# Sliding-window attention and a two-layer MLP on one core: an earlier cast of V, one pair's casts on another engine, masks as factors, and one pair moved by a slot

## Chip, cores, metric

One core of a Trainium2 chip (runs e1 to e9 on one chip, e10 to e13 on another). The metric is the device time of one execution in microseconds (us), measured some 2 us longer than the span of the trace of the same execution. The engines are TensorE (PE in the profile, PEld its weight loads), VectorE (DVE), ScalarE (ACT), GpSimd (POOL) and SyncE (SP, which here only issues DMAs).

## The reference

Eight batches of eight heads, sequence 576, head size 64. Each query sees the 64 latest keys. The attention's output, as 4608 tokens by 512, goes through two matrices with `h - tanh(h)` between.

```python
rel = pos[:, None] - pos[None, :]
mask = (rel >= 0) & (rel < 64)
scores = np.where(mask, scale * q @ k.T, -1e9)
attn = softmax(scores)
x = (attn @ v)            # -> [B*S, H*D] = [4608, 512]
h = x @ w_in              # [4608, 2048]
out = (h - np.tanh(h)) @ w_out
```

## The kernel before

Tokens go through the MLP in nine chunks of 512. A program of numbered slots `h` interleaves the MLP's matmuls (`OPS`) with attention work (`at(h, ...)`). A "pair" `g` is two heads of a batch; pairs 4 to 7 are batch 1 (the second), 8 to 11 batch 2 (the third). Each engine takes its instructions in the order of the program; the framework adds the waits. For one batch, V is loaded (`load_v_all`), cast and rearranged into `vb` (`cast_v`), copied by DMA into 64-key windows `vw` (`keys_v`), and its upper halves are shifted to lower ones (`shift_dve`). `vall` and `vb` have one buffer each, so the load of the next batch's V waits for the cast of this one's.

```python
def move(eng, o, i):                       # line 84 of the profile, 82 for ScalarE
    if eng is nc.scalar: nc.scalar.activation(o, i, ACT.Copy)
    else:                eng.tensor_copy(o, i)
# ... cut ...
def tile_scores(g, grp, banks, how="hide"):
    j0, n = GROUPS[grp]
    if how == "hide":
        hides(grp, banks)                  # 2 matmuls that put -2^30 outside the window (line 259)
    for i in range(n):                     # ... scores of both heads, line 271
        ...
    nc.scalar.activation(o, pair_of(banks)..., ACT.Exp, scale=scale)        # line 274
    if how == "mask":                      # product with 0/1 after exp, line 278
        nc.vector.tensor_tensor(p, p, mask_sb.unsqueeze(1).to_broadcast([128, 2 * n, 64]), ALU.mult)
# ... cut ...
def hp_bank(c, m):                         # bank of a first-layer product
    return m % 3 if c == 0 and m < 6 else m % 2
def hp_mm(c, ms, split):                   # 4 matmuls per m (line 365), then tanh on ScalarE (370)
    ...
def g_sub(c, m):                           # h - tanh(h) on VectorE (377); frees the bank
    ...
# ... cut: items before the change are in the diff below ...
for h in range(32 * NC + 64):
    op = OPS.get(h)                        # h = 0, 2, .. 30: chunk 0, m = h/2;  32 .. 62: chunk 1
    ...                                    # its matmuls (and tanh)
    for fn, args in items.pop(h, []):
        fn(*args)                          # attention work of the slot
    if op and op[0] == "h":
        g_sub(*op[1:])
```

The softmax here doesn't subtract the row's maximum and nothing guards it: scores larger than these inputs give would overflow.

## Time and profile before

| | us |
|---|---|
| time, median of the first 3 runs | 348.37 |
| span of the profiled run | 347.3 |
| TensorE busy, whole span | 321.0 (92%) |
| TensorE idle, 27 to 86 us | 9.8 |
| TensorE idle, 102 to 250 us | 3.3 |

The prediction shows the lines behind this table. Read it by stage, not by the average. Of the 26.3 us in which TensorE idles, 8.8 lie before 27 us, 9.8 between 27 and 86 us, and 7.6 in the 261 us after that. The change works between 27 and 86 us, where the idle time is densest but for the start.

For comparing runs I shall use milestones that can be read from any timeline here: the first subtraction of chunk 0 (VectorE, L377), the first matmul of its m=8, the second half of chunk 1's m=0, chunk 1's m=8 and m=15 (all L365), and the end. They cut the span into six stages; before, these are 30.51, 10.37, 18.96, 12.61, 11.32 and 263.53 us. Of the first stage, no changed instruction is ahead of TensorE's or ScalarE's work, and it varies from run to run.

### The profile page before, as it was taken

Reading aid. Unit: us, or ns where it says so; the run is one execution under the profiler, and the core shown is the slowest. Engines: PE = TensorE matmul, PEld = TensorE weight load, DVE = VectorE, ACT = ScalarE, POOL = GpSimd, SP = SyncE. Lnnn points to the kernel's source line nnn. Section 1 sums busy time; section 2 is a strip of 40 time slices with the busy share of each in tenths; the row PEclk is TensorE's granted clock in tenths of the full one; section 3 lists DMA queues with packets and bytes.
Section 4 is the critical chain, followed back from the end, with each engine's and each line's share of the span. In section 5 each row is a group of like instructions: output and inputs, shape, how many; then the busy total and the mean of one; then the engine's idle time right before and its main releaser. Section 6 shows DMA issues by size and latency. Waiting matters only on the chain.

```text
span 347.3 us, 6279 instructions
## 1 busy us (share of the span) xinstructions
PE 321.0 (92%) x2446; PEld 178.9 (52%) x2476; DVE 197.4 (57%) x324; ACT 189.0 (54%) x344; POOL 111.7 (32%) x160
## 2 busy tenths in 40 slices
PE   6578886888999999999999999999999999999995
PEld 2454554444555555555555555555555444444442
DVE  4575765586345767576676766666666444444400
ACT  3344775756356665666665666666664444444411
POOL 8831559902950814711542276200000000000000
PEclk9558999999999999999999999999999999999999
DMA  8999897996499189749594888244002400110021
GB/s 157 158 175 190 132 153 116 166 204 105 85 160 233 26 144 156 115 88 137 135 164 104 152 142 166 69 101 90 32 31 56 105 30 30 48 45 30 32 85 66
DMA packets 41245, 38.31 MB, mean 110 GB/s; under 512 B 13504, under 2 KB 34496, under 8 KB 41024
## 3 DMA queue, kind: packets, MB, share of 16 engines
q0 software_dynamic: 21296, 19.67, 38.3%
q1 hardware_dynamic: 19568, 17.82, 20.1%
q10 hardware_dynamic: 352, 0.43, 0.4%
q8 instruction: 19, 0.31, 0.4%
q14 instruction: 10, 0.08, 0.1%
HBM read 36.70 MB, written 9.44 MB: 133 GB/s over the span
## 4 chain that ended last, share of the span: by engine, by line
PE 74%; DVE 8%; POOL 5%; ACT 5%; DMA 5%; issue 3%; DVEq 0%; POOLq 0%; ACTq 0%
PE ps L389 35%; PE ps L365 29%; PE ps L315 3%; PE ps L299 3%; DMA qall<-in_q_dram 3%; PE ps L232 3%; DVE gT L377 2%; DMA vall<-in_v_dram 2%; POOL vw L148 1%; DVE xs L326 1%; DVE vw L154 1%; PE ps L332 1%; POOL vb L84 1%; DVE qt L84 1%; ACT th L370 1%
## 5 line engine op out<-in xcount | busy, mean ns | idle before, releaser
L365 PE MATMUL ps<-xT,wi 128*128 128x512 bf16 x576 | 148.2, 381 | 4.3 <-DVE gT L377 3.7
L377 DVE TENSOR_TENSOR gT<-ps,th 128x512 bf16<-128x512 f32 x144 | 98.9, 689 | 79.0 <-ACT th L370 77.2
L389 PE MATMUL ps<-w_out_sb,gT 128*128 128x512 bf16 x547 | 139.2, 379 | 3.0 <-ACT ysb L394 1.5
L370 ACT ACTIVATE th<-ps 128x512 f32<-128x512 f32 x144 | 85.9, 598 | 86.9 <-PE ps L365 83.7
L365 PEld LDWEIGHTS <-wi 128*128 128x128 bf16 x576 | 60.9, 114 | 50.2 <-issue 7.0
L389 PEld LDWEIGHTS <-gT 128*128 128x128 bf16 x576 | 53.4, 98 | 54.8 <-issue 2.8
L301 ACT ACTIVATE pt<-ps 128x384 bf16<-128x384 f32 x66 | 32.3, 490 | 25.5 <-PE ps L299 25.5
L84 POOL COPY vb<-vall 72x1024 bf16<-72x1024 bf16 x24 | 24.8, 1055 | 38.4 <-DMA vall<-in_v_dram 38.4
L84 DVE COPY qt<-ps 64x576 bf16<-64x576 bf16 x22 | 16.7, 760 | 31.0 <-ACT qt L82 31.0
L326 DVE TENSOR_TENSOR xs<-ps,rc 64x576 bf16<-64x576 f32 x44 | 33.2, 755 | 1.1
L394 ACT ACTIVATE ysb<-ps 128x512 f32<-128x512 f32 x36 | 21.5, 598 | 17.3 <-PE ps L389 17.3
L84 POOL COPY qb<-qall 96x768 bf16<-96x768 bf16 x24 | 20.5, 852 | 25.3 <-DMA qall<-in_q_dram 16.9
L315 PEld LDWEIGHTS <-pt 128*128 128x128 bf16 x198 | 16.5, 98 | 14.7
L299 PE MATMUL ps<-qt,kt 128*128 128x128 bf16 x198 | 21.8, 219 | 0.0
L315 PE MATMUL ps<-vw,pt 128*128 128x130 bf16 x198 | 21.8, 220 | 0.0
L84 POOL COPY kb<-kall 96x768 bf16<-96x768 bf16 x24 | 20.5, 853 | 1.3 <-PE ps L232 1.3
L299 PEld LDWEIGHTS <-kt 128*128 128x128 bf16 x198 | 15.5, 98 | 9.2 <-issue 0.3
L82 ACT ACTIVATE kt<-ps 128x576 bf16<-128x576 bf16 x26 | 16.9, 649 | 3.8 <-PE ps L252 2.0
L305 DVE TENSOR_TENSOR pt<-pt,ps 128x1152 bf16<-128x1152 bf16 x22 | 16.4, 745 | 1.7 <-ACT pt L301 1.7
L274 ACT ACTIVATE pt<-ps 128x640 bf16<-128x640 f32 (+1 forms) x20 | 12.6, 648 | 6.0 <-PE ps L271 6.0
L82 ACT ACTIVATE qt<-ps 64x576 bf16<-64x576 bf16 x22 | 14.0, 635 | 1.1 <-PE ps L232 1.1
L148 POOL DMA_DIRECT2D vw<-vb x16 | 9.6, 612 | 8.6 <-DVE vb L84 7.0
(72 smaller groups left out, 196.9 us busy)
## 6 DMA issues: line engine op xcount, KB each, us to landing
out_dram<-ysb SPq DMA_DIRECT2D x36, 256.0 KB
vall<-in_v_dram POOLq DMA_DIRECT2D x7, 576.0 KB, 13.5
qall<-in_q_dram POOLq DMA_DIRECT2D x5, 576.0 KB, 8.4
kall<-in_k_dram POOLq DMA_DIRECT2D x5, 576.0 KB, 8.7
vw<-vb SPq DMA_DIRECT2D x38, 65.0 KB
wi<-in_moe_w_in_dram POOLq DMA_DIRECT2D x2, 1024.0 KB, 15.4
w_out_sb<-in_moe_w_out_dram POOLq DMA_DIRECT2D x2, 1024.0 KB, 12.6
kall<-in_k_dram POOLq DMA_DIRECT2D x11, 144.0 KB, 9.5
```

What stands on the lines that cost most here:

```text
L82: nc.scalar.activation(o, i, ACT.Copy)
L84: eng.tensor_copy(o, i)
L299: nc.tensor.matmul(sp[:, i, :], kT[g % NR][:, 64 * j:64 * j + 128], qT[g % NR][:, :, 64 * j:64 * j + 64], start=True, stop=True)
L301: nc.scalar.activation(PT[g % NPT][:, 3 * grp:3 * grp + 3, :], sp, ACT.Exp, scale=scale)
L305: nc.vector.tensor_tensor(p, p, mask.unsqueeze(1).to_broadcast([128, 2 * NJ, 64]), ALU.mult)
L315: nc.tensor.matmul(ps[:, 5 + grp, 130 * i:130 * i + 130], PT[g % NPT][:, j, :], vw[b % 2][:, j, 2 * pr:2 * pr + 2, :], start=True, stop=True)
L326: nc.vector.tensor_tensor(xo[r, :, :, pr, :], ov[r, :, :, h, 0:D], rc[r].to_broadcast([64, 3, 3, 64]), ALU.mult)
L365: nc.tensor.matmul(hp, w_in_tile(ki, m), chunk_tile(c)[:, :, ki % 2, 64 * (ki // 2):64 * (ki // 2) + 64], start=(ki == 0), stop=(ki == 3))
L370: nc.scalar.activation(th, hp, ACT.Tanh)
L377: nc.vector.tensor_tensor(gT[c][:, m, :], hp, th, ALU.subtract)
L389: nc.tensor.matmul(yp, gT[c][:, m, s * 128:(s + 1) * 128], w_out_sb[:, m, :], start=(m == 0), stop=(m == M - 1))
L394: nc.scalar.activation(ysb, ps[:, yp_bank(c, s), :], ACT.Copy)
```

## The change

The intent is to get batch 2 ready sooner. VectorE casts batch 1's V at slot 1 rather than 11, which lets the window copies and the loads of batch 2 be issued sooner; two memsets go to slot 0; pair 8's casts go from GpSimd (slot 22) to VectorE (slot 27); pairs 8 and 9 are masked by a product after exp instead of by matmuls ahead of the scores, and pair 8's scores come a slot earlier; pair 11's attention starts at slot 57 instead of 58.

```diff
--- before.py
+++ after.py
@@ -492,16 +492,16 @@
         cast(g, "k", eng)
         cast(g, "q", eng)
 
-    at(3, lambda: nc.vector.memset(vw[1][0:64, 0], 0.0))
-    at(3, lambda: nc.vector.memset(qT[1], 0.0))
+    at(0, lambda: nc.vector.memset(vw[1][0:64, 0], 0.0))
+    at(0, lambda: nc.vector.memset(qT[1], 0.0))
+    at(1, lambda: [cast_v(1, pr, V) for pr in range(NP)])
+    at(2, lambda: [keys_v(1, j, (G, Y)[j % 2]) for j in range(NJ)])
     at(8, cast_pair, 4, V)
     at(9, cast_pair, 5, V)
-    at(11, lambda: [cast_v(1, pr, V) for pr in range(NP)])
-    at(12, lambda: [keys_v(1, j, (G, Y)[j % 2]) for j in range(NJ)])
-    at(12, load_v_all, 2)
+    at(2, load_v_all, 2)
     for g in 8, 9, 10, 11:
-        at(12, load, g, "k", G)
-        at(12, load, g, "q", G)
+        at(2, load, g, "k", G)
+        at(2, load, g, "q", G)
     at(16, cast_pair, 6, V)
     at(18, cast_pair, 7, V)
     at(21, shift_dve, 1, 0, 4)
@@ -509,12 +509,12 @@
                                     (5, (13, 14, 15, 15), 2, 3, (4, 5), (6, 7), V),
                                     (6, (17, 18, 20, 21), 2, 3, (4, 5), (4, 5), A),
                                     (7, (19, 20, 23, 24), 2, 3, (4, 5), (4, 5), A),
-                                    (8, (29, 30, 34, 36), 3, 2, (4, 5), (4, 5), A),
+                                    (8, (29, 30, 33, 35), 3, 2, (4, 5), (4, 5), A),
                                     (9, (36, 37, 41, 43), 3, 2, (4, 5), (4, 5), A)):
         at(t[0], tr_rows, g, "k", ka, eng)
         at(t[1], tr_rows, g, "q", qa, A)
-        at(t[2], tile_scores, g, 0, a)
-        at(t[3], tile_scores, g, 1, b)
+        at(t[2], tile_scores, g, 0, a, "hide" if g < 8 else "mask")
+        at(t[3], tile_scores, g, 1, b, "hide" if g < 8 else "mask")
     for pr in range(NP):
         at(22 + 2 * pr, tile_pv, 4 + pr, (6, 7))
     at(27, x_tr, 1, 0, 0, 4, 3, A)
@@ -522,7 +522,7 @@
     at(30, x_tr, 1, 1, 0, 4, 7, V)
     at(31, x_tr, 1, 1, 4, 9, 4, A)
     at(21, lambda: [cast_v(2, pr) for pr in range(NP)])
-    at(22, cast_pair, 8, G)
+    at(27, cast_pair, 8, V)
     at(23, lambda: [keys_v(2, j, (G, Y)[j % 2]) for j in range(NJ)])
     at(23, load_w_out, 0)
     at(23, load_w_out, 1)
@@ -541,7 +541,7 @@
     at(78, x_tr, 2, 1, 4, 9, 3, A)
 
     LOADS = {4: (75, 77, 79), 5: (106, 109, 102), 6: (140, 144, 126), 7: (168, 171, 158)}
-    STEPS = {2: (0, 0, 49, 58), 3: (72, 79, 86, 93), 4: (100, 107, 114, 121), 5: (128, 135, 142, 149)}
+    STEPS = {2: (0, 0, 49, 57), 3: (72, 79, 86, 93), 4: (100, 107, 114, 121), 5: (128, 135, 142, 149)}
     TURNS = {13: (97, 3, 99, 3), 15: (110, 4, 111, 3)}
     VALUES = {3: (66, 1, 71), 4: (88, 1, 93), 5: (110, 2, 120), 6: (132, 5, 150), 7: (164, 5, 182)}
     for g in range(2 * NP + 2, B * NP):
```

## The prediction

> **How the program is laid out.** The body runs through numbered slots. In slots 0 to 30 the even ones hold the first layer of chunk 0 (m = slot/2), in 32 to 62 the first layer of chunk 1; slots 64 to 79 hold chunk 0's second layer, and from 80 on first and second layers alternate. Attention work for later batches is hung on slots; each engine takes its instructions strictly in this order, and in a slot the attention items come before the slot's subtraction on VectorE.
>
> **What bounds the kernel now.** I began with the page's busy times (us, share of the span, instructions): TensorE (PE) leads by far.
>
> ```profile
> PE 321.0 (92%) x2446; PEld 178.9 (52%) x2476; DVE 197.4 (57%) x324; ACT 189.0 (54%) x344; POOL 111.7 (32%) x160
> ```
>
> Then a table of engine times by stage. Columns are the stage in us, its length, then busy us and instruction counts of TensorE, its weight loads, VectorE, ScalarE, GpSimd, then granted clock, DMA share and GB/s:
>
> ```profile
> 27.00:44.00 17.00, 14.48 (x129) 7.75 (x127) 11.62 (x27) 10.84 (x20) 6.60 (x10) 0.94 1.04 158
> 44.00:58.00 14.00, 11.05 (x173) 6.42 (x170) 9.17 (x16) 8.75 (x16) 9.85 (x14) 1.00 0.95 136
> 58.00:70.00 12.00, 10.07 (x117) 5.92 (x115) 6.71 (x10) 8.98 (x17) 11.92 (x16) 1.00 0.91 159
> 70.00:86.00 16.00, 13.56 (x115) 7.82 (x116) 11.56 (x19) 10.42 (x20) 1.72 (x2) 1.00 0.96 160
> 86.00:102.00 16.00, 15.94 (x113) 8.71 (x113) 5.55 (x10) 5.70 (x12) 14.05 (x22) 1.00 0.63 102
> 102.00:250.00 148.00, 144.67 (x1077) 84.14 (x1095) 101.10 (x158) 94.56 (x180) 49.99 (x66) 1.00 0.66 124
> ```
>
> From 86 us on TensorE is busy 98 to 100% and sets the end, so whatever is saved before 86 us should arrive at the end one for one. Between 27 and 86 us TensorE idles 2.52 + 2.95 + 1.93 + 2.44 = 9.8 us; the whole change works there. 9.8 us (2.8%) is its ceiling, and only if no idle time at all remained.
>
> Next the timeline of TensorE, for its gaps (start, length, what ran; in brackets the idle time before and who ended it):
>
> ```profile
> 54.16 0.45 PE L332 MATMUL ps<-ident,xs 128*128 128x128 bf16 x5
> 56.93 0.43 PE L252 MATMUL ps<-ident,kb 96*128 96x96 bf16 x6 [2.32 <-POOL kb L84]
> ...
> 83.77 1.02 PE L365 MATMUL ps<-xT,wi 128*128 128x512 bf16 x4 [1.56 <-DVE gT L377]
> ```
>
> The largest gap, 2.32 us, ends when GpSimd has cast pair 8's keys. Then the timeline of GpSimd, for why that is so late:
>
> ```profile
> 38.66 3.33 POOL L148 DMA_DIRECT2D vw<-vb  x5 [7.02 <-DVE vb L84]
> 41.96 0.86 POOL L118 DMA_DIRECT2D vall<-in_v_dram  x1
> ...
> 51.45 0.63 POOL L95 DMA_DIRECT2D qall<-in_q_dram  x1 [4.16 <-DMA vall<-in_v_dram]
> 52.07 4.03 POOL L84 COPY vb<-vall 72x1024 bf16<-72x1024 bf16 x4
> 56.05 0.82 POOL L84 COPY kb<-kall 96x768 bf16<-96x768 bf16 x1
> ```
>
> So the gap hangs on a chain: VectorE's cast of batch 1's V (36.95 to 38.37), the copies into the windows of V, the load of batch 2's V (issued 41.96, landed 9.2 us later), its cast on GpSimd, and only then pair 8. The second gap, 1.56 us, is VectorE's: its half of the copy of pair 11's q, which waits for ScalarE's half, stands ahead of the subtraction that frees TensorE's bank.
>
> ```profile
> 82.23 0.76 DVE L84 COPY qt<-ps 64x576 bf16<-64x576 bf16 x1 [1.56 <-ACT qt L82]
> 83.02 0.69 DVE L377 TENSOR_TENSOR gT<-ps,th 128x512 bf16<-128x512 f32 x1
> ```
>
> **What the Trainium skill says.** "VectorE: DVE Perf Modes", Rules for kernel authors: 16-bit dense copies in SBUF get the 4x rate, tensor_tensor 2x. The trace agrees in kind: the 96x768 cast takes 344 ns on VectorE against 853 on GpSimd, while a 128x640 masking product takes 492. "SBUF — State Buffer", Who interferes with whom: such copies and GpSimd's instructions lock each other out of a shared port pair. The trace shows it: two 64x2080 shifts took 2.19 us at 67.05, beside GpSimd's casts, but 1.38 at 46.40, beside DMA issues alone. "DMA: Bandwidth & Descriptors", Issuing engines are not separate DMA queues: transfers from any engine share the same 16 DMA engines, so V copies that start earlier compete with what is still on the way; here the DMA share is 0.97 or more from 27 to 35 us and 36 to 38 us, and falls to 0.45 at 39 to 40.
>
> **The change part by part, on the path of TensorE.**
>
> (a) The two memsets (31.85 to 32.87, 1.0 us of VectorE) go to slot 0, where VectorE waits 3.43 us for the first tanh: free. The V cast (4 copies, 1.42 us) goes from slot 11 to slot 1. Its input must have landed: issued 14.60, 15.3 us to landing, so 29.9; the cast would start at about 31.2, a margin of 1.3 us. VectorE has no idle time from 30.5 to 40.7, so order matters more than sum. Walking it with the durations of the trace: the subtraction of m=1 ends at 33.2 (was 31.8), so the matmuls of m=4 wait from 32.3 to 33.24; m=2's at 33.85 (33.5), m=5's matmuls end at about 34.96 (34.4); pair 4's keys come out of PSUM at 36.95 (36.4), pair 5's q at 40.5 (40.03). So the matmuls of m=8 start at 41.35 instead of 40.88: TensorE loses about **0.45 us**. The later saving of the 1.42 us and of the memsets is spent by then.
>
> (b) The V copies can be issued from 32.6 on (38.66), but not all: each of GpSimd's DMA issues waits for the eighth before it to land. The fourth copy stands behind the second half of w_in (18.16 + 19.4 = 37.6), and batch 2's V behind a load that lands at 39.0, both somewhat later with the earlier copies beside them. I put V's issue at 40.0 (41.96), landing at 49.2 (51.2), its cast at 49.9 to 53.95 (56.1).
>
> (c) Pair 8's casts on VectorE: 0.34 + 0.35 us, about 0.65 pipelined, after the subtraction of m=13 (ends 54.25 + 0.45). GpSimd's cast of V should just be over, so they run undisturbed. Keys are there at about 55.0; TensorE finishes its transposes at 54.6 + 0.45, so it goes straight on. The price is that the normalisation of pair 7 moves back 0.65 us and with it the last transposes of batch 1: from my walk they start at 56.0 + 0.45 (were 58.32). The second half of chunk 1's m=0 starts at 57.4 + 0.45 = 57.85, was 59.84: **2.0 us net** gained by (a) to (c).
>
> (d) Masks of pairs 8 and 9: TensorE loses 8 matmuls of mask (2 x (0.43 + 0.38) = 1.6 us in the timeline), VectorE gains 4 products, 2 x (0.49 + 0.43) = 1.84 us. Does it help? The stretch from m=0 to m=8 of chunk 1 (60.45 to 72.45, 12.0 us) is not held by TensorE's work but by two banks in turn (matmuls, tanh, subtraction) and the 2.19 us shift at slot 40. TensorE gets ahead at first (m=5 starts 5.55 us after the start of the stretch instead of 6.6), but then the shift, two products and two normalisations queue up on VectorE: m=8 starts after 11.65. Gain **0.35 us**, the freed TensorE time turned into waiting.
>
> (e) Pair 11 at slot 57 instead of 58: ScalarE's half of the q copy now comes ahead of the next tanh, VectorE's half beside that tanh, not after it. The subtraction of m=13 ends at 82.4 instead of 83.7, m=15's matmuls start at 82.46 instead of 83.77: **1.3 us**.
>
> Sum: -0.45 + 2.45 + 0.35 + 1.3 = 3.65 us, where 2.45 is (c) before the loss of (a). 348.37 - 3.65 = 344.7; I say **345.0**, as such walks leave out small new waits.
>
> **Rivals.** (1) A new wait takes the place of the old one: pair 9's keys still come from GpSimd behind V, its copies, w_out and a q load. My times give keys at 60.1, q at 60.9; TensorE wants them at 60.85 and 61.1. If V lands no earlier than before, GpSimd only saves pair 8's casts (1.6 us) and TensorE waits over 1 us there; gain about 2 us, 346.3. For it: those DMA issues wait on a w_in transfer that doesn't move. Against: DMA has a trough from 39 to 46 us (0.45 to 1.00, mostly under 0.85) to fill. (2) VectorE becomes the bound: the cast of pair 8 is locked out by GpSimd's V cast (up to 1.05 us a copy), and the products hold up subtractions; then (c) gives 1 us and (d) loses 0.5: 347. For: margin in (c) is only 0.7 us. Against: VectorE is busy only 56 to 72% of these stages. (3) Batch 1's V lands after slot 1 in some runs: VectorE stands, and all of chunk 0's start with it, one for one; with 1 us late, 345.7. (4) All gaps behave: an undisturbed shift (0.8 us less) and no loss in (a) give 343.3.
>
> **Range and chances.** Rivals 2 and 4 mark the ends: 343.2 to 347.2 for 8 in 10. Faster by over 2% means under 341.5, 6.9 us of 9.8 us idle: 0.03. Slower by over 2% would need a lost 7 us, for which I see no source: 0.01. Within 2%: 0.96.
>
> **What would show it.** Right: no wait for GpSimd's keys near 55 us; memsets before the first subtraction at no cost; the first V cast at about 31 us without a wait; batch 2's V issued about 40, landed about 49; TensorE idle before chunk 0's m=4 of about 1 us; the 1.56 us gap before m=15 down to some 0.2; TensorE's gap-free stretch starting near 82.5 instead of 85. Wrong: a wait of over 0.5 us for pair 9's keys, pair 8's casts over 0.6 us each, a wait for V's DMA ahead of the first cast, or a later stage (102 to 250 us) longer than 148 us for the same work.

## The result, and the profile after

The changed kernel took 344.53 us (median of 6 runs, 343.08 to 351.76) against 348.73 for the kernel before (6 runs, 347.94 to 351.01); the ratio of the fast runs is 0.9853, interval 0.9811 to 0.9895: faster by about 1.5%, clear of noise and under 2%. A ratio here is the mean time of one kernel's fast runs over that of the other's of the same rounds, so it isn't quite the ratio of the medians quoted. A fast run is one within 1.5% of the kernel's fastest. Of the six, two were slow (351.76 and 349.44), and the first profile happened to be one of these. So I ran the changed kernel again first (below) and read the result from that profile, which is fast: time 343.96, span 341.9 us.

The table by stage of the changed kernel's fast run, with the columns and the edges of the prediction's table:

```profile
27.00:44.00 17.00, 14.06 (x130) 7.86 (x128) 11.71 (x25) 11.01 (x20) 8.71 (x14) 1.00 1.08 173
44.00:58.00 14.00, 12.96 (x197) 7.58 (x196) 10.49 (x20) 10.55 (x20) 11.71 (x16) 1.00 0.98 152
58.00:70.00 12.00, 9.70 (x113) 5.45 (x113) 10.17 (x17) 7.52 (x14) 6.10 (x8) 1.00 1.03 188
70.00:86.00 16.00, 15.36 (x114) 8.57 (x111) 11.15 (x18) 10.14 (x21) 6.11 (x7) 1.00 0.67 115
```

These edges are fixed times, so the same row holds somewhat different work before and after. TensorE is 1.9 us busier from 44 to 58 us and 1.8 us busier from 70 to 86 us. VectorE is at 85% from 58 to 70 us (56% before): there the masks are.

The timeline of TensorE, changed kernel, fast run:

```profile
31.78 1.89 PE L365 MATMUL ps<-xT,wi 128*128 128x512 bf16 x8 [1.07 <-DVE gT L377]
...
52.97 0.45 PE L332 MATMUL ps<-ident,xs 128*128 128x128 bf16 x5
53.39 0.43 PE L252 MATMUL ps<-ident,kb 96*128 96x96 bf16 x6
...
78.32 1.02 PE L365 MATMUL ps<-xT,wi 128*128 128x512 bf16 x4 [0.39 <-DVE gT L377]
```

The 2.32 us gap before pair 8's keys is gone (second and third line), the 1.56 us gap before m=15 is 0.39, and the foreseen new wait of about 1 us for the matmuls of chunk 0's m=4 is 1.07. The timeline of GpSimd of the same run:

```profile
31.45 2.12 POOL L148 DMA_DIRECT2D vw<-vb  x3 [0.54 <-DVE vb L84]
37.06 0.55 POOL L148 DMA_DIRECT2D vw<-vb  x1 [3.49 <-DMA wi<-in_moe_w_in_dram]
38.02 0.55 POOL L148 DMA_DIRECT2D vw<-vb  x1 [0.40 <-DMA kall<-in_k_dram]
39.36 0.84 POOL L118 DMA_DIRECT2D vall<-in_v_dram  x1 [0.79 <-DMA qall<-in_q_dram]
...
47.75 4.03 POOL L84 COPY vb<-vall 72x1024 bf16<-72x1024 bf16 x4
```

As foreseen, the fourth window copy waits for the second half of w_in (3.49 us), and V's load for one more landing. It is issued at 39.36, 2.6 us sooner than before, and its cast starts at 47.75, 4.3 us sooner.

The stages of all profiles, in us (each row adds up to its span):

| kernel | to first subtraction | to m=8 | to chunk 1's m=0 | to its m=8 | to its m=15 | to the end | span |
|---|---|---|---|---|---|---|---|
| before | 30.51 | 10.37 | 18.96 | 12.61 | 11.32 | 263.53 | 347.3 |
| before again (e9) | 28.28 | 10.36 | 20.36 | 12.56 | 11.32 | 263.52 | 346.4 |
| odd slot alone (e4) | 30.63 | 10.37 | 19.21 | 12.61 | 9.97 | 263.51 | 346.3 |
| masks alone (e5) | 29.07 | 10.36 | 19.76 | 13.33 | 11.31 | 263.57 | 347.4 |
| pair 8 alone (e3) | 29.84 | 10.37 | 17.91 | 11.97 | 11.32 | 263.49 | 344.9 |
| V first alone (e2) | 28.59 | 11.04 | 16.43 | 12.16 | 11.32 | 263.56 | 343.1 |
| changed (e1) | 28.94 | 10.86 | 16.49 | 12.06 | 9.97 | 263.58 | 341.9 |
| changed, no masks (e6) | 28.97 | 11.11 | 16.59 | 11.42 | 9.97 | 263.54 | 341.6 |
| changed, pair 8 back (e12) | 31.14 | 10.71 | 16.47 | 12.06 | 9.97 | 263.55 | 343.9 |
| changed, guard (e7) | 28.34 | 11.34 | 17.48 | 13.10 | 9.97 | 263.47 | 343.7 |
| changed, late (e10) | 29.52 | 10.73 | 16.63 | 11.11 | 9.97 | 263.54 | 341.5 |
| changed, late, guard (e11) | 31.32 | 10.71 | 16.49 | 11.65 | 9.97 | 263.56 | 343.7 |
| casts after shift (e13), slow | 31.39 | 10.70 | 20.63 | 11.00 | 9.97 | 263.51 | 347.2 |
| changed, first profile, slow | 32.81 | 10.71 | 21.66 | 11.12 | 9.97 | 263.53 | 349.8 |

The last stage is 263.5 us in all fourteen, within 0.1. So what is saved or lost before m=15 of chunk 1 arrives at the end one for one, and the rest of the question is about the four stages in the middle.

### The profile page after: what moved, and what is told of

Read it like the earlier page. It is cut to its first block, busy times and chain, and to the rows that moved or that the text cites. A ratio compares the mean times of both kernels' runs of the same rounds, so it can differ in the third digit from the quotient of the medians.

```text
span 349.8 us, 6270 instructions
## 1 busy us (share of the span) xinstructions
PE 322.8 (92%) x2438; PEld 179.2 (51%) x2468; DVE 202.2 (58%) x330; ACT 188.5 (54%) x344; POOL 110.1 (31%) x158
## 4 chain that ended last, share of the span: by engine, by line
PE 74%; DVE 10%; DMA 7%; ACT 4%; issue 2%; POOL 1%; ACTq 0%; DVEq 0%; POOLq 0%
PE ps L389 34%; PE ps L365 29%; PE ps L315 3%; PE ps L299 3%; DMA vw<-vb 3%; PE ps L232 3%; DMA kall<-in_k_dram 2%; DVE gT L377 2%; DVE vw L154 2%; DMA vall<-in_v_dram 2%; DVE xs L293 2%; DVE xs L326 1%; PE ps L332 1%; DVE qt L84 1%; ACT th L370 1%
## 5 line engine op out<-in xcount | busy, mean ns | idle before, releaser
L84 POOL COPY qb<-qall 96x768 bf16<-96x768 bf16 x23 | 19.2, 835 | 29.1 <-DMA qall<-in_q_dram 23.1
L84 POOL COPY kb<-kall 96x768 bf16<-96x768 bf16 x23 | 19.3, 837 | 2.5 <-PE ps L232 2.5
L82 ACT ACTIVATE xT<-ps 128x512 bf16<-128x512 bf16 (+3 forms) x18 | 7.2, 453 | 10.9 <-PE ps L332 10.8
```

## Experiments

The starts of single profiles differ by up to 3 us (first column), so the stages tell parts apart that the times can't.

### e1: the changed kernel again

No edit.

> The changed kernel once more, unaltered, for a profile in the fast state and for its spread. Its first profile was slow (351.8 us) and shows two losses that I did not foresee: 2.75 us in which VectorE's first shift of V (batch 0) waits for a DMA near 20 us, and a shift of batch 1 that takes 5.00 us near 49 us (1.38 before) while GpSimd casts batch 2's V. Theory: the second follows from the first. When the start runs late by about 3 us, the shift falls upon GpSimd's four casts, which come earlier now, and is locked out. Then a fast run (343 to 345 us) has neither loss, its shift takes 1.3 to 1.5 us and GpSimd's cast starts after it; a slow run has both. Rival 1: the shift is locked out in fast runs too (some 5 us), and what makes a run slow is something else, such as the clock. Rival 2: the slow runs are slow at the end, past 90 us.

344.15 us (343.64 to 345.71, no slow run among 6) against 349.54; ratio 0.9864, 0.983 to 0.9898. The profile agrees with the collision theory: the wait of 2.75 us near 20 us is not there, its shift of batch 1 takes 1.31 us and ends at 46.5, and GpSimd's casts begin at 47.75. In the first, slow profile the shift runs into the casts. Here VectorE's, TensorE's and GpSimd's lines of the slow run:

```profile
48.94 5.00 DVE L154 COPY vw<-vw 64x2080 bf16<-64x2080 bf16 x2
53.38 0.32 PE L287 MATMUL ps<-vw,pt 128*64 128x65 bf16 x8 [2.77 <-DVE vw L154]
48.76 4.02 POOL L84 COPY vb<-vall 72x1024 bf16<-72x1024 bf16 x4
```

The first of the two shifts starts 0.18 us after GpSimd's first cast and ends at 53.33, 0.55 us after GpSimd's fourth; the second takes 0.68 us, as elsewhere. TensorE stands 2.77 us. Rival 2 is out: the late part of the slow run (263.53 us) is as everywhere. Rival 1 is out as far as the shift goes, but the clock has a part: the granted clock of the slow profile is 0.50 from 54.7 to 58.1 us, soon after the stand, and four matmuls of the first layer take 1.89 us there, elsewhere 1.03 to 1.05. Whether the stand brings that drop is not shown by a run of its own; e13 and e9 have the same drop of 3.4 us soon after their stands of 2.10 and 3.03 us, and the kernel before none after 2.32. The stage from m=8 to chunk 1's m=0 is 21.66 us instead of 16.49, collision and clock together; the later start accounts for another 3.9 us of the 7.9 between the two spans.

### e2: V first alone

```diff
+    at(0, lambda: nc.vector.memset(vw[1][0:64, 0], 0.0))       # both memsets from slot 3
+    at(1, lambda: [cast_v(1, pr, V) for pr in range(NP)])      # from slot 11
+    at(2, ...)                                                 # keys_v, load_v_all, loads of pairs 8-11 from 12
```

> The first part alone: memsets at slot 0, V's cast at slot 1, window copies and loads at slot 2; pair 8 stays on GpSimd, masks and slots as before. My prediction's walk: TensorE loses 0.45 us before the matmuls of m=8, GpSimd is 2.0 us earlier with V, so pair 8's keys come at about 54.9 rather than 56.9 and the gap of 2.32 us nearly goes: gain about 1.8 us, 346.6 to 346.9 against 348.5. Rival: without the cast on VectorE nothing is gained, since the window copies stand behind the second half of w_in: within 0.5 us of before. Slow runs with the long shift should appear here too, as V's cast is as early as in the whole change.

345.36 us (344.56 to 348.17), ratio 0.9907 (0.9869 to 0.9945): this part alone brings most of the gain, and more than the 1.8 us that I expected. Against the first profile of before, TensorE loses 0.67 us up to m=8, then wins 2.53 us in the next stage and 0.45 in the one after. The rival (nothing without the cast on VectorE) is out. No long shift showed in this profile (1.31 us), and no run was slow by the 1.5% rule.

### e3: pair 8 on VectorE alone

```diff
-    at(22, cast_pair, 8, G)
+    at(27, cast_pair, 8, V)
```

> Pair 8's casts on VectorE at slot 27 alone, V as late as before. If GpSimd's queue alone made the gap, it goes: the keys and queries have landed by 52.6, gain 2 us or more. If the port lock counts, VectorE's two casts meet GpSimd's V cast (52.07 to 56.1) and take 1 us and more instead of 0.35, gain only 0.5 to 1.2 us; then the early V is what makes the cast on VectorE pay. I lean to the second: about 347.5.

347.31 us (346.76 to 349.04), ratio 0.9956 (0.9923 to 0.9989). The stage from m=8 to chunk 1's m=0 is 1.05 us shorter than in the first profile of before, and the next is 0.64 us shorter, as the waits of 0.30 and 0.33 us for pair 9's keys and queries are gone. The lock shows, VectorE first, then GpSimd, then TensorE:

```profile
53.50 1.66 DVE L84 COPY kb<-kall 96x768 bf16<-96x768 bf16 x1
50.91 4.03 POOL L84 COPY vb<-vall 72x1024 bf16<-72x1024 bf16 x4
55.21 0.43 PE L252 MATMUL ps<-ident,kb 96*128 96x96 bf16 x6 [1.27 <-DVE kb L84]
```

The first cast takes 1.66 us instead of 0.34 and ends just after GpSimd's last (54.94); TensorE still waits 1.27 us, now for VectorE. Moving the work to another engine did not take it out of GpSimd's way.

### e4: the odd slot alone

```diff
-    STEPS = {2: (0, 0, 49, 58), ...}
+    STEPS = {2: (0, 0, 49, 57), ...}
```

> Pair 11 at slot 57 instead of 58 alone. Prediction: the gap of 1.56 us before chunk 0's last... precisely, before chunk 1's m=15 falls to about 0.2, gain 1.3 us, 347.2. Rival: TensorE is held further on by the next subtraction or mask (pair 10's masking comes ahead of two subtractions), and only 0.5 us or less arrives at the end.

348.24 us (346.57 to 348.53), ratio 0.9965 (0.9933 to 0.9996). The stage from m=8 to m=15 of chunk 1 is 9.97 us, not 11.32: 1.35 us won, and the last stage unchanged, so it all arrives. (The forecast of 347.2 us was worked out from 348.5; the kernel before had 349.54.) VectorE's lines of the fast run of the changed kernel (e1), which has the same slot:

```profile
75.88 0.69 DVE L377 TENSOR_TENSOR gT<-ps,th 128x512 bf16<-128x512 f32 x1 [0.40 <-ACT th L370]
76.79 0.76 DVE L84 COPY qt<-ps 64x576 bf16<-64x576 bf16 x1 [0.21 <-ACT qt L82]
77.58 0.69 DVE L377 TENSOR_TENSOR gT<-ps,th 128x512 bf16<-128x512 f32 x1
```

The copy of q waits 0.21 us for ScalarE's half instead of 1.56. All nine profiles with the odd slot have 9.97 us, all five without it 11.31 or 11.32.

### e5: the masks alone

```diff
+    at(t[2], tile_scores, g, 0, a, "hide" if g < 8 else "mask")    # slots 33, 35 for pair 8, was 34, 36
```

> Masks of pairs 8 and 9 as factors, one slot earlier, alone. Prediction: the stretch from chunk 1's second half of m=0 to its m=8 (12.61 us in the profile of before) gets some 0.35 us shorter, as the two banks and VectorE hold it and not TensorE's matmuls; here perhaps less, since pair 9's keys still come late from GpSimd. Rival: TensorE's 1.6 us of mask matmuls count in full, 11.0 us. Rival: VectorE's 1.84 us of products count, stretch longer. Everything else as before; time 0.2 to 0.4 us under before, within the noise of the start.

349.34 us (347.8 to 351.23), ratio 1.0015 (0.9978 to 1.0052): no gain. The stretch is 13.33 us against 12.61 and 12.56, so it is the last rival that fits best in the trace: longer, though by less than the products' 1.84 us. Part of it are waits of 0.60 and 0.55 us for pair 9's keys and queries from GpSimd (0.30 and 0.33 before).

### e6: the changed kernel without the masks

```diff
-    at(t[2], tile_scores, g, 0, a, "hide" if g < 8 else "mask")
+    at(t[2], tile_scores, g, 0, a)                                  # slots 34, 36 again
```

> The changed kernel with the masks of pairs 8 and 9 as before (hide, slots 34, 36, 41, 43). By the stages of the last call the masks are worth 0.55 us at most: 344.2 to 344.7 against 344.2 for the whole change. The other stages should stay as they are in the whole change (16.5 us from m=8 to chunk 1's m=0, 9.97 us up to m=15).

343.88 us (343.22 to 346.76), ratio 0.987 (0.9834 to 0.9906), against 0.9864 with the masks: the same. Its stretch is 11.42 us, shorter than e1's 12.06. So the times show nothing that the masks add to the change. Why not, shows on VectorE in e1:

```profile
58.16 1.27 DVE L278 TENSOR_TENSOR pt<-pt,mask_sb 128x640 bf16<-128x640 bf16 x1
59.96 0.44 DVE L278 TENSOR_TENSOR pt<-pt,mask_sb 128x512 bf16<-128x512 bf16 x1
...
62.50 2.16 DVE L154 COPY vw<-vw 64x2080 bf16<-64x2080 bf16 x2
```

The first product takes 1.27 us, not 0.48, and overlaps GpSimd's casts of pair 9 (57.33 to 58.97). In e7 one of the shorter products took 2.16 us beside such casts; it ended 0.8 us after the last of them, so not all of that is shown to be theirs. The shift then overlaps GpSimd's casts of pair 11. Both stand in the row of subtractions that free TensorE's banks.

The stretch goes with this shift, and not with the masks. It is 11.00 to 11.12 us where the shift takes 1.31 us (e13, e10, first profile), 11.42 and 11.65 where it takes 1.72 and 1.84 (e6, e11), and 12.06 to 12.16 where it takes 2.16 to 2.21 (e1, e12, e2); e13, e6 and e2 of these have no mask products. Only e7, with its product of 2.16 us and a wait of 0.63 us for pair 9's keys, departs (13.10 at 2.18). The shift of e6, then that of e10, which starts as GpSimd's last cast ends (63.02):

```profile
63.15 1.72 DVE L154 COPY vw<-vw 64x2080 bf16<-64x2080 bf16 x2
62.99 1.31 DVE L154 COPY vw<-vw 64x2080 bf16<-64x2080 bf16 x2
```

### e7: a guard ahead of GpSimd's casts

```diff
+    at(21, lambda: nc.gpsimd.tensor_copy(tick, vw[1][0:1, NJ - 1, 0, 0:1]))   # waits for the shift
     at(21, lambda: [cast_v(2, pr) for pr in range(NP)])
```

> The changed kernel plus one 1x1 copy on GpSimd ahead of its cast of batch 2's V, which reads what VectorE's second shift of batch 1 writes, so that the casts can't start before the shifts are over. Theory of the collision: in fast runs no change (shifts end at 46.5, V lands at 47.1), 344.2; slow runs lose their extra 3.6 us, so that no run is above 348 or so. Rival: slow runs stay as slow (349 to 352), since the late start alone makes them.

344.41 us (343.69 to 345.49), ratio 0.9876 (0.9847 to 0.9905). No slow run among six, but e1 and e6 had none either, so the times alone don't decide. In this profile V landed late (10.0 us after its issue, 7.5 in e1), so that the guard had nothing to hold back; the casts of pair 8 on VectorE then overlapped GpSimd's casts of V and took 0.69 and 1.21 us. So the profile does not test the theory.

### e9: the kernel before against itself

No edit.

> The kernel before, unaltered, against itself: a null test, ratio 1 within its interval, and a second profile of its start. Five profiles have the first matmul of chunk 0 at 25.96 to 27.38 us (29.68 in the slow one), before any changed instruction: if that is luck, the kernel before should also show starts of 26.0 here. From the first subtraction on the stages should be as in its first profile: 10.37, 18.96, 12.61, 11.32 and 263.5 us, within 0.3.

348.0 us (346.18 to 350.24), ratio 0.9975 (0.9939 to 1.0012): the same program against itself came out 0.25% apart, within an interval of 0.37% to either side. Against this the times of e3 (0.9956) and e4 (0.9965) alone would prove little; their stages decide. The start is earlier than in the first profile (28.28 us), as I had expected. One stage is not within 0.3 us: from m=8 to chunk 1's m=0 it has 20.36 us, 1.4 more. TensorE and GpSimd of this run:

```profile
55.30 0.43 PE L252 MATMUL ps<-ident,kb 96*128 96x96 bf16 x6 [3.03 <-POOL kb L84]
39.45 0.86 POOL L118 DMA_DIRECT2D vall<-in_v_dram  x1
49.83 0.63 POOL L95 DMA_DIRECT2D qall<-in_q_dram  x1 [4.93 <-DMA vall<-in_v_dram]
```

So in the kernel before, 0.7 us of an early start are given back in the gap (3.03 us instead of 2.32). The other 0.7 us fall where the granted clock is 0.50 (56.1 to 59.6 us); in the first profile it is 1.00 there, and the six transposes of pair 8's queries take 0.42 us, here 0.69. V is issued here as early as in the changed kernel (39.45, there 39.36), yet lands 10.1 us later, there 7.5. The window copies go out shortly ahead of it here; in the changed kernel three of GpSimd's five have been issued by 33.6. That this is the reason is not shown: e7 issues them as early, and its V needed 10.0 us.

### e10 and e11: a start made late on purpose, without and with the guard

```diff
-    warm(2)
+    warm(11)          # 9 more idle matmuls ahead of the last transposes of the start
```

> The changed kernel with 9 more idle matmuls ahead of the last transposes of the start, which hold TensorE up by some 3 us at about 25 us and leave the transfers alone: the slow state made on purpose. Collision theory: V of batch 2 still lands near 47 to 48 us, VectorE's shift of batch 1 comes to about 48 us, among GpSimd's four casts; it takes 3 to 5 us instead of 1.3, and the kernel loses its 3 us and another 2 to 3.6: about 349 to 351. Rival: only the 3 us (or less, if the start has slack) are lost, 346 to 347.3, shift 1.3 to 1.5 us.

> The same late start, with the 1x1 copy that keeps GpSimd's casts behind the shift. Collision theory: shift 1.3 to 1.5 us, casts after it, 346.5 to 348, at least 1.5 us faster than the late start without it. Rival: no difference between the two.

e10: 344.8 us (343.2 to 351.76), ratio 0.9891 (0.9853 to 0.9929); four runs 343.2 to 345.0, two slow, 351.6 and 351.8. e11: 345.39 us (344.2 to 346.57), ratio 0.9912 (0.9881 to 0.9942), none slow. They were run on another chip. The edit did not do what I meant: the first subtraction of e10's profile is at 29.52, only 0.6 us after e1's, so it isn't 3 us late, its shift (1.31 us) doesn't collide, and the forecast of 349 to 351 for all runs failed. So did that of e11, to be 1.5 us faster than e10. Two slow runs in six fit the theory without proving it. All runs together say more: six of the 41 runs with early V and no guard of the shift of batch 1 were slow, none of the 63 without early V, and none of the 12 with the guard. So the slow runs come with the early V; that the guard removes them is likely but open, since 12 runs at that rate would be free of slow ones by chance about once in seven (an estimate from these counts). The profile of e11 did start late (31.32) and shows the guard at work, GpSimd first, then VectorE:

```profile
48.95 0.18 POOL L524 COPY tick<-vw 1x1 bf16<-1x1 bf16 x1 [1.17 <-DVE vw L154]
49.63 4.03 POOL L84 COPY vb<-vall 72x1024 bf16<-72x1024 bf16 x4 [0.51 <-issue]
47.44 1.44 DVE L154 COPY vw<-vw 64x2080 bf16<-64x2080 bf16 x2
```

GpSimd waited 1.17 us for the shift, which took 1.44 us. Without this guard e13, which starts as late (31.39), has 4.33. A late start alone does not bring the collision: e12 starts at 31.14 and has 1.31, as its V lands at 48.3 and not at 45.7 as in e13. In these profiles it takes a landing that is early for the start.

### e12: pair 8 back on GpSimd

```diff
-    at(27, cast_pair, 8, V)
+    at(22, cast_pair, 8, G)
```

> The changed kernel with pair 8's casts back on GpSimd at slot 22. V first alone already has 16.43 us from m=8 to chunk 1's m=0 against 16.49 for the whole change, so the cast on VectorE should be worth nothing in a fast run: 344.0 to 344.6. Rival, my prediction's reading that the two parts work together: 1 us or more slower, 345.3 and up.

345.78 us (344.72 to 351.14, one slow), ratio 0.9925 (0.9891 to 0.9958). The stages say no difference (16.47 against 16.49, all others alike). The time missed my 344.0 to 344.6 and is where the rival put it: 1 to 2 us slower than e1, e6 and e7, which ran on the other chip, and 1 us slower than e10; but this profile began 2.2 us later than e1's, ahead of anything changed. It remains unclear: a start that happened to be late in these runs, or runs in which V landed late, where GpSimd's cast of pair 8 would hold TensorE up and VectorE's doesn't.

### e13: GpSimd's casts of pairs 10 and 11 behind the shift of batch 2

```diff
-    at(24, cast_pair, 10, G)
-    at(38, cast_pair, 11, G)
     at(40, shift_dve, 2, 0, 4)
+    at(40, lambda: nc.gpsimd.tensor_copy(tick, vw[0][0:1, NJ - 1, 0, 0:1]))
+    at(40, cast_pair, 10, G)
+    at(40, cast_pair, 11, G)         # on the changed kernel without the masks
```

> The changed kernel without the mask products, and GpSimd's casts of pairs 10 and 11 put behind VectorE's shift of batch 2 (a 1x1 copy that reads what the shift wrote). If the port pair is what stretches that shift (1.7 to 2.6 us in nine profiles, 1.31 in one), it takes 1.3 us here, the stretch from chunk 1's m=0 to m=8 falls from 11.42 to about 11.0, and the time to 343.4 or so. Rival: pair 10's keys, now cast at about 65 us, come late for slot 49, and the gain is lost there.

343.37 us (342.84 to 349.3, one slow of 5), ratio 0.9857 (0.9822 to 0.9891): the lowest median, though its interval contains the changed kernel's 0.9864. It was run on another chip. The profile is of the slow run, and shows both effects on VectorE:

```profile
47.50 4.33 DVE L154 COPY vw<-vw 64x2080 bf16<-64x2080 bf16 x2
...
69.19 1.31 DVE L154 COPY vw<-vw 64x2080 bf16<-64x2080 bf16 x2
```

The unguarded shift of batch 1 collides (4.33 us; GpSimd casts V from 46.64 to 50.67), the guarded one of batch 2 takes 1.31 us, and its stretch of 11.00 us is the shortest of all, as expected, though by 0.12 us only: in e10 and the first profile the shift of batch 2 fell clear of the casts by itself (1.31 us), and they have 11.12 with the masks. Both guards together would be the version to build next; it was not run.

## Why the prediction was right

The time on record was 345.0 us and the measured 344.53. The early V and the odd slot did what the prediction says; the masks did not, and part of the agreement in size is luck. By its steps:

- **What bounds the kernel.** Right. The last stage is 263.5 us in all fourteen profiles.
- **(a) memsets and cast.** Predicted a loss of 0.45 us up to m=8; the nine profiles with the early cast, fast or slow, show 10.70 to 11.34 against 10.37, a loss of 0.33 to 0.97, 0.49 in e1. The memsets cost nothing. The cast of V found its data landed in seven of the nine profiles; in e6 and e7 it waited, so rival 3 came true in small, and e7, then e6, have the largest losses (11.34 and 11.11):

```profile
29.95 1.45 DVE L84 COPY vb<-vall 72x1024 bf16<-72x1024 bf16 x4 [0.29 <-DMA vall<-in_v_dram]
29.55 1.45 DVE L84 COPY vb<-vall 72x1024 bf16<-72x1024 bf16 x4 [0.52 <-DMA vall<-in_v_dram]
```

- **(b) V earlier.** Right in kind and cautious in size. Issue predicted at 40.0, measured 39.36; landing predicted at 49.2, measured 46.8 (39.36 + 7.5). I had foreseen only an earlier issue, with 9.2 us to landing as before. With early V the landing took 7.2 to 8.4 us in seven profiles, 9.3 and 10.0 in the other two; without it 8.7 to 10.1 in five. That the window copies are no longer beside the load would explain it, but is not shown (see e9).
- **(c) pair 8.** The sum of (b) and (c), 2.45 us, is what the trace has: 18.96 to 16.49. That it fits so closely is in part luck, as V landed 2.4 us sooner than predicted and the profiles of before differ by 1.4 us in this stage. And the share of the cast on VectorE is not shown: e2 without it has 16.43, e12 16.47. Early V alone closes the gap. On its own, the cast on VectorE brought 1.05 us, since it meets GpSimd's casts (e3): that lock was rival 2, and it is real.
- **(d) masks.** The wrong step. I gave it 0.35 us; e5 gives none (ratio 1.0015) and e6 without it is as fast as e1 with it. I took the products at 0.49 and 0.43 us, the values at the start, where GpSimd casts nothing. In this stretch GpSimd casts pairs 9 to 11, and a product took up to 2.16 us. That the stretch got shorter all the same (12.06 against 12.61) goes back to GpSimd being earlier: e2 has 12.16 without masks. What sets it is how much of the shift of batch 2 falls upon GpSimd's casts (e6), which I had taken as 2.19 us whatever happens.
- **(e) odd slot.** Predicted 1.3 us, measured 1.35, in each of nine profiles.

The sum predicted was 3.65 us. Pooled, 45 runs of the kernel before have a mean of 348.77 us and the 10 fast runs of the changed kernel 344.18: 4.6 us (5.1 and 4.9 us within the rounds of the result and of e1). The stages account for most of it if all profiles are used and not only the one I worked from. From the first subtraction to chunk 1's m=0, the four kernels without early V and without pair 8 on VectorE (before, e9, e4, e5) need 29.94 us on average, the seven fast ones with early V (e1, e2, e6, e7, e10, e11, e12) 27.58: 2.4 us. The next stage brings 0.6 (12.59 for before, e9 and e4; 12.00 for the five fast profiles with early V and masks), and the odd slot 1.35: 4.3 us. So the gain was larger than the 3.65 of the walk, and 345.0 fits as well as it does within a spread of starts of 3 us.

Of the prediction's signs of being wrong, none stands in e1. In e7, where V landed at 49.5 us, three of the four do: a wait of 0.63 us for pair 9's keys, casts of pair 8 of 0.69 and 1.21 us, and a wait of 0.52 us ahead of the first cast of V. Its run is a fast one all the same (345.49 us), though the slowest of e7.

**What I missed.** The early V cast brings GpSimd's four casts near VectorE's shift of batch 1, which was clear of them before by 4.3 us (47.78 to 52.07). In both slow profiles of kernels with early V they collide, and the stage is 4.1 and 5.2 us longer than in e1, part of it at half the clock. I had read the lock in the trace and looked for it at pair 8 only. Whether every slow run is such a collision is not shown, as only two were traced, and the comparison of the two kernels doesn't rest on them.

## What to carry to other kernels

An earlier transfer moves everything that waits for it on the other engines too: list what the released engine will do next, and beside what. When two engines lock each other out, as VectorE's and GpSimd's copies did here, take an instruction's cost from a place in the trace where the other engine is doing what it will be doing. And read a gain from stages between milestones in several profiles: a gap that ends with a landing can swallow part of an early start (0.7 of 2.2 us in e9), so one profile of the kernel before gives one value of the gain only. Look at the granted clock of each stage too, before a longer stage is put down to waits alone.

## What the Trainium skill lacked or had wrong

- "SBUF — State Buffer", Who interferes with whom: the runs agree with it where I had not applied it. It says that a VectorE instruction with two SBUF inputs contends with GpSimd instructions that read SBUF; the masking products, 0.48 and 0.42 us alone, took 1.27 us (e1) and 2.16 us (e7) beside GpSimd's casts. It does not say what a row of GpSimd instructions does: one copy of a shift did not end before all of four casts on end were over, and took 3.72 us (e13) and 4.39 us (slow run), against 0.70 alone.
- "DMA: Bandwidth & Descriptors", Issuing engines are not separate DMA queues: the section says that all share the engines and interleave, which no run here tests by itself, and gives no figure for a load beside others. The same 576 KB load of batch 2's V landed 7.2 to 10.1 us after its issue over the fourteen profiles; what decides between them is not shown.
- No page has what held GpSimd's issues up here: in this program each of its DMA issues waits for the eighth before it to land (3.49 us for w_in in e1).
- "TensorE: Matmul & The Clock Gate", Part 1, says that the warm-up varies from run to run. The runs agree: the changed kernel was granted 0.50 of the clock from 9.7 to 26.8 us in e1 and 1.00 in these stages of the first profile, and the slower of the two runs was the one with the full clock at its start.
